# One written order for a fused attention and two-MoE kernel, with subtractions placed one by one and the last output tile sent in halves

## The chip, the cores and the metric

The kernel runs on one core of a Trainium2 chip. The metric is device time in microseconds, the median of repeated executions. The engines named below are TensorE (PE; its weight loads are shown as PEld), VectorE (DVE), ScalarE (ACT), GpSimd (POOL) and SyncE (SP), which here only issues DMAs.

## The reference, cut to what matters

Three stages follow one another; q, k, p are scaled by 8 from the drawn inputs.

```
attention   q, k, v: (8 batches, 8 heads, 576, 64); p: (8, 8, 32, 64)
   packed = softmax(p k^T / 8) v
   x = softmax(q packed^T / 8) packed      -> 4608 tokens x 512
first MoE   h = x w_in (512 x 2048);  g = h * sigmoid(1.702 h);  x = g w_out (2048 x 512)
second MoE  out = (silu(x w_gate) * (x w_val)) w_out (512 x 1536, 512 x 1536, 1536 x 512)
```

All of it is float32. The weights arrive as 64-bit words and are converted on the chip.

## The kernel before, in words

**Precision.** A float32 operand is held as two fp32r tiles, a high part and a rest. `high` (L453) is an ACT copy into the high half, `rest` (L456) a subtraction, source minus high, on the engine that it is given. `mm3` (L465) makes one product from three matmuls. So each operand of TensorE costs one ACT copy and one subtraction; the change speaks of these subtractions.

**First part, eight batches.** A batch has 32 units (two halves of 288 tokens, 16 blocks of 128 hidden columns). Unit n runs `p1` (6 matmuls of 288 columns into `h`), `tanh` on ACT, `gate` on VectorE, `hi` (ACT copy to `gh`) and `lo` (the subtraction), and, three units later, `p2` (12 matmuls of 288 columns into the four `acc` banks). Batch b's units run while batch b+1's attention is computed in between: `do_T`, `sc1`, `max1`, `exp1`, `a1T`, `pv`, `sc2`, `max2`, `exp2`, `norm2`, and last `do_z` (L831), eight times: `zm` (4 matmuls of 512 columns into `zp`, from tiles `wh` that `win` loads), `zc` on ACT and `za` on VectorE, which empty the bank, then `zh` and `zl`. `zp` has two PSUM banks, which it shares with attention's other products; `wh` has three buffers. At the end of a half the four `acc` banks are halved into `x` and stored (L900).

**In the same stretch** two blocks of side work prepare the second MoE: the last batch has no attention, and there `sums` (L1046) and `prep` (L991) form sums of weight tiles in `ws` on VectorE, split them and store them (`w5s`, `w2s`).

**Second part.** One tile of 512 tokens is done directly (`single`, L1285), then four pairs of tiles by a scheme with seven products instead of eight. A pair has 12 units: seven products `pr j 0..6` (6 matmuls of 512 columns each into `gv`), and element work c1, e1 ... g2 on ACT and VectorE. Then come 42 steps `pt n`, each in two halves of 3 matmuls into `acc`, on operands made by `hi n`, `lo n` from the tiles that `SUMS` (L928) names for n. `fd` (L1218) empties an `acc` bank, on ACT for its first group and on VectorE for the others; `tr` transposes a finished tile and `od` (L1234) sends a quarter of it. The next pair's inputs are loaded (`lx`) and split (`xa`, `xh`, `xl`) during the `pt` steps.

**What sets the order.** `FIRST` (the opening, to batch 0's end) and `SECOND` (the four pairs) are texts of steps, carried out by `issue` (L1318); while `pin["on"]` holds, each engine keeps the order of the text. Between them, from batch 1's first unit to the end of the direct tile, `pin` is off (L1329 to L1385): a loop calls the steps, `STEADY` says which attention steps go with which unit, and the framework's own scheduler arranges each engine's instructions.

Of the kernel before, what the change touches and what calls it, by code (L numbers as in the profile page):

```python
# [18 lines left out]
FIRST = """  # L19
    load_raw 0; pad_F 0; make_consts; do_T 0 0; do_T 0 1; load_p 0; load_raw 1; do_p; stage in 3; rebias in 3; stage  # L20
    in 2; warm 12; stage out 1; do_T 1 0; do_T 1 1; load_raw 2; rebias in 2; warm 8; warm 2; sc1 0; max1 0; low in 3
    dve; low out 1 dve; exp1 0; warm 8; warm 5; sc1 1; norm1 0; max1 1; stage in 1; rebias in 1; exp1 1; do_T 2 0;
# [7 lines left out]
    store_w 0 sp; low in 4 dve; rebias in 4; oh 0; join out 2; tanh 1; rebias in 8; oh 2; ol 2 pool; join in 4; tanh  # L30
    0; warm 6; zm 2; ol 0 pool; stage in 7; low in 7 act; rebias in 7; gate 1; max2 1 1; hi 1; lo 1 pool; stage out
    3; stage in 9; zh 2; join in 7; p1 3; exp2 1 1; sc2 0 1; gate 0; stage out 7; tanh 3; zl 2 dve; norm2 1 1; low
    in 8 act; join in 8; low out 3 act; p1 2; stage out 6; store_w 2 sp; rebias out 3; join out 3; tanh 2; hi 0; lo
    0 pool; zm 3; zh 3; rebias out 7; gate 2; hi 2; p2 0; stage in 11; low in 9 dve; zl 3 dve; max2 0 1; load_p 1;
    rebias out 6; stage in 10; low in 11 act; rebias in 9; p1 5; stage in 13; gate 3; hi 3; lo 2 pool; p2 2; join in
    9; rebias in 11; stage in 12; join in 11; zm 4; tanh 5; low out 6 act; join out 6; gate 5; p1 6; rebias in 10;
    lo 3 pool; store_w 3 sp; stage out 10; low in 10 dve; zh 4; oh 3; low out 7 dve; stage out 5; oh 6; join in 10;
    ol 3 pool; join out 7; zl 4 dve; p1 4; tanh 4; gate 4; low in 13 act; low in 12 dve; zm 5; p2 3; oh 7; +do_p;
    rebias in 12; join in 12; zh 5; ol 6 dve; stage in 15; hi 4; p2 1; lo 4 pool; zl 5 dve; p1 9; ol 7 pool; tanh 6;
# [5 lines left out]
    act; zh 7; zl 7 dve; oh 4; tanh 7; exp2 0 1; gate 7; load_raw 5; hi 7; ol 10 pool; +do_T 1 0; +do_T 1 1; +sc1 0;
    +max1 0; tanh 11; p1 10; ol 4 pool; ah 1 1; hi 9; stage out 13; rebias out 13; low out 13 act; p2 4; join out
    13; store_w 5 sp; +exp1 0; lo 7 pool; p2 7; rebias out 9; gate 11; norm2 0 1; join out 9; lo 9 pool; stage out
    11; tanh 10; oh 8; hi 11; lo 11 pool; oh 13; load_v 1 0; ol 8 dve; load_raw 6; store_w 6 sp; gate 10; low out 11
    dve; p1 12; ol 13 dve; stage out 15; tanh 12; rebias out 11; join out 11; gate 12; +sc1 1; hi 10; oh 9; ah 0 1;
    +win 0; p1 13; tanh 13; oh 11; ol 11 pool; p2 8; lo 10 dve; hi 12; lo 12 pool; +max1 1; +exp1 1; p1 14; ol 9  # L50
    pool; stage out 12; gate 13; +norm1 0; p2 10; +do_T 2 0; tanh 14; +do_T 2 1; p2 11; +win 2; hi 13; +a1T 0; gate
    14; wch 0; wcl 0 dve; al 0 1 pool; rebias out 12; load_v 1 1; al 1 1 dve; hi 14; rebias out 15; +copy_a1T 0; low
    out 12 dve; join out 12; p2 9; p1 17; low out 15 act; join out 15; oh 12; p1 16; lo 13 dve; +pv 0; ol 12 dve; p2
    13; tanh 16; wch 2; wcl 2 pool; stage out 14; +norm1 1; tanh 17; oh 15; gate 16; +do_D 0 act; +do_E 0; +a1T 1;
    low out 14 act; +copy_a1T 1; rebias out 14; store_w 7 sp; p1 15; tanh 15; +pv 1; +win 1; join out 14; hi 16; ol
    15 pool; wst 2; oh 14; lo 14 dve; gate 15; ol 14 dve; +split_E 0; p1 21; +zm 0 0; hi 15; wch 1; wcl 1 dve; wst
    0; lo 16 dve; +zc 0 0; +za 0 0; p2 12; +sc2 0 0; tanh 21; gate 21; p1 20; lo 15 dve; +win 3; +do_D 1 act; +do_E
    1; hi 21; p2 14; lo 21 pool; +max2 0 0; +raw_ahead 1; gate 17; +zm 0 1; wch 3; p1 22; +win 5; wst 1; +split_E 1;
    +exp2 0 0; wcl 3 dve; +zc 0 1; +raw_ahead 0; +zm 1 0; +zc 1 0; +win 8; +norm2 0 0; +win 4; wst 3; hi 17; +za 1
    0; tanh 22; gate 22; lo 17 pool; wch 5; +za 0 1; tanh 20; p2 15; wcl 5 dve; wst 5; hi 22; +zm 1 1; +zh 0; +zl 0  # L60
    pool; p1 19; lo 22 dve; tanh 19; gate 19; +zc 1 1; +za 1 1; wch 4; p2 16; p2 17; +zh 1; +zm 2 1; wcl 4 dve; gate
    20; p1 18; hi 20; +zl 1 pool; wch 8; wcl 8 dve; +win 6; hi 19; wst 4; +zm 2 0; tanh 18; lo 19 dve; gate 18; +win
    7; +zc 2 0; +za 2 0; wch 6; +win 10; +zc 2 1; p2 22; p1 25; wcl 6 pool; wst 6; p1 23; tanh 23; +do_T 3 0; +do_T
    3 1; lo 20 pool; +za 2 1; +zh 2; gate 23; +sc2 0 1; +max2 0 1; +sc2 1 0; hi 18; p2 21; tanh 25; wst 8; wch 7;
    wcl 7 dve; +zl 2 pool; hi 23; +zm 3 0; lo 23 pool; +max2 1 0; +zc 3 0; +za 3 0; +win 9; p1 26; p2 19; +zm 3 1;
    tanh 26; gate 25; lo 18 pool; gate 26; +zm 4 0; wch 10; +exp2 0 1; wcl 10 dve; hi 26; lo 26 dve; +win 11; wch 9;
    wcl 9 dve; +zc 3 1; p1 24; wst 7; +win 12; tanh 24; wst 9; +zc 4 0; +za 3 1; +zh 3; p2 26; p2 23; wch 11; +sc2 1
    1; wcl 11 pool; +norm2 0 1; +za 4 0; hi 25; lo 25 pool; +ah 0 1; p1 27; gate 24; +exp2 1 0; +zm 4 1; p1 30; hi
    24; lo 24 pool; +max2 1 1; +ah 0 0; +zl 3 dve; +zm 5 0; p2 20; wch 12; wcl 12 pool; +zc 4 1; +za 4 1; +win 13;
# [1350 lines left out]
```

## Time and profile before

| | |
|---|---|
| median of 3 runs | 1626.05 us (1625.08 to 1627.06) |
| the profiled execution | 1625.42 us, span 1623.7 us |
| PE busy | 1591.4 us, 98% |
| DVE, ACT, POOL busy | 81%, 50%, 24% |
| chain that ended last | PE 81%, DVE 8%, issue 4%, DMA 3% |
| DMA | 349.89 MB, mean 215 GB/s |

The span is the time from the first to the last instruction. The profile's busy time of TensorE takes a modelled end for each matmul, longer than the spacing of matmuls that run without a stop. All source lines are L338 in the trace, since one helper records every operation; rows are told apart by the tile names, written out<-in.

### The profile page before, as it was taken

Reading aid. Unit: us, or ns where it says so; the run is one execution under the profiler, and the core shown is the slowest. Engines: PE = TensorE matmul, PEld = TensorE weight load, DVE = VectorE, ACT = ScalarE, POOL = GpSimd, SP = SyncE. Lnnn points to the kernel's source line nnn. Section 1 sums busy time; section 2 is a strip of 40 time slices with the busy share of each in tenths; the row PEclk is TensorE's granted clock in tenths of the full one; section 3 lists DMA queues with packets and bytes.
Section 4 is the critical chain, followed back from the end, with each engine's and each line's share of the span. In section 5 each row is a group of like instructions: output and inputs, shape, how many; then the busy total and the mean of one; then the engine's idle time right before and its main releaser. Section 6 shows DMA issues by size and latency. Waiting matters only on the chain.

```text
span 1623.7 us, 26484 instructions
## 1 busy us (share of the span) xinstructions
PE 1591.4 (98%) x9202; PEld 1421.3 (88%) x9202; DVE 1312.8 (81%) x2356; ACT 803.9 (50%) x1717; POOL 396.4 (24%) x319
## 2 busy tenths in 40 slices
PE   8999999999999999999999999999999999999997
PEld 7799999999999999999988888778887888788886
DVE  7988787777868778688789388899889988998894
ACT  5876667565665756566554222442235222532241
POOL 1333131230312213124231111241114111321142
PEclk9999999999999999999999999999999999999999
DMA  9987657475664747247899485668567866676627
GB/s 311 321 272 231 195 174 247 140 235 156 210 204 150 228 126 241 88 162 257 301 350 351 144 327 190 207 202 259 188 205 222 204 244 198 198 209 225 198 83 167
DMA packets 254565, 349.89 MB, mean 215 GB/s; under 512 B 127968, under 2 KB 169952, under 8 KB 254432
## 3 DMA queue, kind: packets, MB, share of 16 engines
q1 hardware_dynamic: 252320, 347.94, 67.1%
q8 instruction: 73, 1.20, 0.3%
q14 instruction: 60, 0.49, 0.1%
q10 hardware_dynamic: 2112, 0.26, 0.1%
HBM read 274.20 MB, written 73.92 MB: 214 GB/s over the span
## 4 chain that ended last, share of the span: by engine, by line
PE 81%; DVE 8%; issue 4%; DMA 3%; ACT 2%; SPq 1%; POOL 1%; ACTq 0%; POOLq 0%; DVEq 0%
PE acc L338 32%; PE gv L338 30%; PE h L338 10%; PE sc L338 3%; PE zp L338 3%; PE pv L338 2%; DVE z L338 1%; DMA x<-x2d 1%; DVE g L338 1%; DVE gh L338 1%; PE idle L338 1%; SPq L338 1%; DVE c L338 1%; ACT z L338 1%; DVE x L338 1%
## 5 line engine op out<-in xcount | busy, mean ns | idle before, releaser
L338 PE MATMUL gv<-xh,w 128*128 128x512 f32 x2304 | 537.8, 389 | 0.8 <-DMA w<-w2s 0.8
L338 PEld LDWEIGHTS gv<-xh,w 128*128 128x128 f32 x2304 | 432.3, 188 | 90.9 <-DVE c L338 1.2
L338 PE MATMUL acc<-gh,wo 128*128 128x288 f32 x3072 | 456.1, 297 | 2.6 <-DVE x L338 2.2
L338 PEld LDWEIGHTS acc<-gh,wo 128*128 128x128 f32 x3072 | 426.4, 189 | 7.4 <-DVE x L338 2.4
L338 POOL TENSOR_TENSOR gh<-g,gh 128x512 fp32r<-128x512 f32 (+1 forms) x124 | 171.2, 1384 | 556.6 <-ACT gh L338 485.6
L338 ACT CAST gh<-g 128x288 fp32r<-128x288 f32 (+1 forms) x418 | 208.1, 505 | 163.7 <-DVE g L338 118.2
L338 PE MATMUL h<-a,z 128*128 128x288 f32 x1536 | 252.2, 299 | 1.2 <-DVE g L338 1.0
L338 PE MATMUL acc<-gh,w 128*128 128x512 f32 x972 | 236.7, 390 | 6.1 <-ACT c L338 3.8
L338 DVE TENSOR_TENSOR gh<-g,gh 128x288 fp32r<-128x288 f32 (+1 forms) x294 | 192.8, 656 | 54.0 <-ACT gh L338 50.8
L338 PEld LDWEIGHTS h<-a,z 128*128 128x128 f32 x1536 | 221.0, 189 | 10.4 <-DVE g L338 3.2
L338 PEld LDWEIGHTS acc<-gh,w 128*128 128x128 f32 x972 | 181.5, 188 | 47.6 <-ACT c L338 5.2
L338 DVE TENSOR_TENSOR c<-gv,c 128x512 f32<-128x512 f32 x192 | 131.7, 688 | 20.2 <-ACT tb L338 11.9
L338 DVE SCALAR_TENSOR_TENSOR g<-sig,h 128x288 f32<-128x288 f32 x256 | 114.0, 446 | 36.6 <-ACT sig L338 33.8
L338 ACT ACTIVATE sig<-h 128x288 f32<-128x288 f32 x256 | 104.2, 408 | 68.9 <-PE h L338 66.7
L338 ACT COPY tb<-gv 128x512 f32<-128x512 f32 x48 | 28.2, 587 | 202.7 <-PE gv L338 202.7
L338 POOL TENSOR_TENSOR z<-z,z 128x512 fp32r<-128x512 f32 x51 | 69.7, 1368 | 150.9 <-ACT z L338 150.9
L338 DVE TENSOR_TENSOR z<-zp,z 64x512 f32<-64x512 f32 (+1 forms) x120 | 81.9, 683 | 14.1 <-ACT z L338 11.2
L338 DVE TENSOR_TENSOR ta<-gv,c 128x512 f32<-128x512 f32 x96 | 65.8, 685 | 20.9 <-PE gv L338 20.6
L338 ACT COPY c<-gv 128x512 f32<-128x512 f32 x48 | 28.2, 587 | 107.4 <-PE gv L338 92.5
L338 PE MATMUL zp<-wh,E 128*128 128x512 f32 x224 | 66.7, 400 | 4.4 <-DVE z L338 2.4
L338 ACT COPY z<-zp 64x512 f32<-64x512 f32 x112 | 65.1, 581 | 11.6 <-PE zp L338 8.9
L338 DVE TENSOR_TENSOR g<-g,g 128x512 f32<-128x512 f32 x96 | 68.2, 741 | 0.1
(153 smaller groups left out, 1735.8 us busy)
## 6 DMA issues: line engine op xcount, KB each, us to landing
w<-w2s SPq DMA_DIRECT2D x144, 512.0 KB, 4.4
wh<-win SPq DMA_DIRECT2D x96, 512.0 KB, 4.1
w<-w5s SPq DMA_DIRECT2D x84, 512.0 KB, 4.4
w2s<-w SPq DMA_DIRECT2D x36, 512.0 KB, 5.6
w<-w2s SPq DMA_DIRECT2D x48, 256.0 KB, 2.7
vt<-in_v_dram SPq DMA_DIRECT2D x80, 128.0 KB, 3.3
x2d<-x SPq DMA_DIRECT2D x16, 576.0 KB, 3.2
w2d<-f SPq DMA_DIRECT2D x36, 256.0 KB, 3.0
```

The source lines that it names most:

```text
L338: x = getattr(self.engine, name)(*a, **k)
```

## The change

`STEADY` and the loops go. `FIRST` stays as it was but for the halving and the store of batch 0's first half, which now stand as steps of their own. Twelve further texts, `REST`, hold 5,633 steps: seven for batches 1 to 7, one for the direct tile and four for the pairs. Each step names whose it is (`a3.` is batch 3's attention, `p0.` the first pair), and all are pinned. To make that possible the helpers are cut into single steps: `split_T` into `th` and `tl`, `combine` into four `cb`, `sums` into `sq`, `sh`, `sl`, `sd`, `prep` into `wh2`, `wl2`, `wd2`, the halving into `hv` and its store into `sx`, `single` into `sg`, `st2`, `su2`, `sm2`, `gh2`, `gl2`. The code of each is what stood in the helper, and each subtraction takes its engine from the text.

Counted over the texts, the subtractions on GpSimd are 19 in a batch's attention before and after (batches 3 to 6), and 24 of the sums and 12 of the direct tile before and after; in a pair's first 12 `lo` they were all on GpSimd and are now 5 or 6 on GpSimd and 6 or 7 on VectorE. The same matmuls are made, but for the last output tile.

`SUMS` changes its order, and the last tile has half steps:

```
-    SUMS = [(j % 2, j // 2) for j in range(NM2)] + [(j, k) for j in range(2, 7) for k in range(NK)]
+    SUMS = [(j % 2, j // 2) for j in range(NM2 - 4)] + [(j, k) for j in range(2) for k in range(NK - 2, NK)] + \
+        [(j, k) for j in range(2, 7) for k in range(NK)]
...
+        def pth(n, h):
+            k = n - 36
+            if (k, h) == (0, 0):
+                ab[1] = ps_acc.tile([P, 512], F32, tag="acc1", name="acc")
+            w, y, s = w5[p, n // 2][:, n % 2], oper[p, n], slice(256 * h, 256 * h + 256)
+            mm3(ab[1][:, s], lambda a: w[:, a, P:2 * P], lambda c: y[:, c, s], k == 0, k == NK - 1)
+
+        def fdh(h):
+            s = slice(256 * h, 256 * h + 256)
+            fold(where(6, 1)[0][:, s], ab[1][:, s], c2[:, s])
...
-        def od(j, e, a):
+        def od(j, e, a, eng, h=None):
...
-                    eng = ACT if p == NPAIR - 1 and j == 6 and a % 2 else SP
                     eng.dma_start(out=out[b * S:(b + 1) * S].rearrange("(i n) e -> i n e", n=NBLK)[:, k:k + c, e0:e0 + 32],
                                   in_=y[:, t:t + c])
```

With `SUMS` as it is now, group 0 of the `pt` steps ends at n=9 and group 1 at n=11; before, they ended at n=10 and n=11. Group 2 begins at n=12 in both.

The texts at the places that matter (before, then after; the owner, such as `p0.`, is left out of the pairs' new texts):

```
-    28: "do_z 4; win 13; win 14",
-    30: "do_z 5",
-    31: "do_z 6; win 15; do_z 7",
...
+    a2.win 11; a2.zc 4 0; a2.ah 1 1; a2.za 4 0; a2.al 1 1 pool; a2.zm 4 1; gate 61; a3.do_T 1 1; p1 62; a2.win 12;
+    a2.zc 4 1; hi 61; a2.zm 5 0; a2.za 4 1; a3.raw_ahead 2; p2 59; ...
+    p1 64; lo 63 pool; a2.zm 5 1; p2 61; ... p1 66; ... a2.zm 6 1 ... p1 67; ... a2.zm 7 0; ... a2.zm 7 1; ... p1 68;
...
+    p1 243; hv 239 1 dve; lo2 1; hv 239 0 act; hv 239 2 act; hv 239 3 dve; sh 4 2; lo 242 dve; p2 240; sx 239; ...
...
+    sd 5 2; sh 5 1; oh2 2; cb 0 2; sl 5 1 pool; od2 1; p2 244; ol2 2 dve; tanh 247; sd 5 1; gate 247; sh 5 0;
...
-    pr 11 6; hi 11; xa 0 0; lw5 8; hi 14; b5 11; lx 5; xh 0 4; lo 14 dve; lo 11 pool; pt 10 0; ... pt 10 1; fd 0 0;
-    e5 11; pt 11 0; t2 11; ... pt 12 0; lw5 9; lo 15 pool; fd 0 1; hi 16; pt 12 1;
+    pt 9 1; hi 11; b5 11; lx 5; fd 0 0; pr 11 6; ... pt 10 0; ... e6 11; ... pt 11 0; t2 11; ... pt 12 0; fd 0 1; lw5 9;
+    hi 16; pt 12 1;
...
-    lx 6; pt 26 0; hi 30; lw5 16; lx 7; pt 26 1; xa 1 0; pt 27 0; ... pt 28 0; xh 1 6; lw5 17; hi 32; pt 28 1; xa 1 1;
+    lx 6; fd 3 0; pt 26 0; xl 0 5; lw5 16; hi 30; lx 7; ... pt 29 1; xh 1 4; lo 32 dve; lo 33 pool; xh 1 6; pt 30 0; ...
+    pt 33 0; hi 37; xa 1 1;
...
-    fd 6 1; od 6 0 0; od 6 0 2; tr 6 1; od 6 1 0; od 6 1 1; od 6 1 2; od 6 1 3
+    pth 41 0; od 5 1 3 act; fdh 0; od 6 0 0 sp; pth 36 1; tr 6 1 0; pth 37 1; od 6 0 1 act; od 6 0 2 sp; pth 38 1;
+    od 6 0 3 act; pth 39 1; od 6 1 0 sp 0; pth 40 1; od 6 1 1 act 0; pth 41 1; od 6 1 2 sp 0; od 6 1 3 act 0; fdh 1;
+    tr 6 1 1; od 6 1 0 sp 1; od 6 1 1 act 1; od 6 1 2 sp 1; od 6 1 3 act 1
```

The weight loads of the first pair (`lw 0 0` to `lw 2 1`) stand in the new text ahead of the stores of the direct tile's output; before, `lw 1 0` and the following stood behind them.

## Rows read from the trace of the kernel before

**Rows 1.** The page: busy time, share of the span, instructions of each engine.

```profile
PE 1591.4 (98%) x9202; PEld 1421.3 (88%) x9202; DVE 1312.8 (81%) x2356; ACT 803.9 (50%) x1717; POOL 396.4 (24%) x319
```

**Rows 2.** Windows: stretch, its length, busy us of each engine, clock, DMA.

```profile
148.10:240.00 91.90, 88.68 (x648) 85.90 (x647) 70.45 (x161) 53.08 (x127) 17.98 (x16) 1.00 0.61 182
240.00:760.00 520.00, 517.38 (x3795) 507.57 (x3794) 401.13 (x876) 325.52 (x767) 123.94 (x104) 1.00 0.58 186
760.00:795.00 35.00, 32.09 (x213) 31.01 (x212) 27.33 (x55) 19.18 (x50) 15.73 (x19) 0.90 0.87 299
...
919.00:935.00 16.00, 15.17 (x68) 12.23 (x67) 8.87 (x14) 4.32 (x8) 1.81 (x1) 1.00 0.76 250
...
1050.00:1095.00 45.00, 42.99 (x186) 34.23 (x185) 42.89 (x54) 22.04 (x38) 20.26 (x14) 1.00 0.70 209
1095.00:1225.00 130.00, 130.00 (x575) 107.64 (x574) 110.86 (x164) 38.96 (x68) 19.17 (x13) 1.00 0.70 216
1225.00:1260.00 35.00, 32.81 (x144) 26.50 (x143) 32.81 (x40) 19.48 (x34) 17.23 (x12) 1.00 0.72 220
...
1400.00:1435.00 35.00, 33.17 (x145) 26.85 (x144) 33.16 (x41) 19.02 (x33) 18.55 (x13) 1.00 0.70 210
```

**Rows 3.** Waits of PE, 148.1 to 1615: us in total, times, longest.

```profile
PE acc L338 <- ACT c L338: 3.8, 3, 1.3
PE zp L338 <- DVE z L338: 2.4, 4, 1.1
...
PE acc L338 <- DVE gh L338: 2.0, 3, 0.9
PE zp L338 <- DMA wh<-win: 1.7, 4, 0.7
```

**Rows 4.** Timeline and one window around 780: start, us, instruction, idle before it.

```profile
755.40 1.75 PE L338 MATMUL acc<-gh,wo 128*128 128x288 f32 x12
...
779.95 1.82 DVE L338 TENSOR_TENSOR ws<-w 128x256 f32<-128x256 f32 x2 [0.45 <-POOL tb L338]
...
783.79 2.53 PE L338 MATMUL acc<-gh,wo 128*128 128x288 f32 x9 [2.19 <-DVE x L338]
787.55 2.83 PE L338 MATMUL acc<-gh,wo 128*128 128x288 f32 x12
...
785.00:790.00 5.00, 5.00 (x23) 5.00 (x23) 4.40 (x11) 2.36 (x5) 0.00 (x0) 0.51 0.80 238
```

**Rows 5.** Timeline, 919 to 931: the first pair's weights.

```profile
919.81 9.00 PE L338 MATMUL gv<-xh,w 128*128 128x512 f32 x39
...
923.00 2.31 SPq L338 DMA_DIRECT2D out_dram<-g  x5
...
929.65 5.72 PE L338 MATMUL gv<-xh,w 128*128 128x512 f32 x24 [0.83 <-DMA w<-w2s]
```

**Rows 6.** Timeline, 1226 to 1260: the second pair's pt steps.

```profile
1226.81 0.60 ACT L338 ACTIVATE c<-acc 128x512 f32<-128x512 f32 x1
...
1252.17 0.62 ACT L338 CAST xh<-x 128x512 fp32r<-128x512 f32 x1 [2.89 <-DMA x<-x2d]
```

**Rows 7.** DVE groups, 1095 to 1225: busy us, mean ns, idle before.

```profile
L338 DVE TENSOR_TENSOR c<-gv,c 128x512 f32<-128x512 f32 x48 | 32.9, 688 | 5.0 <-ACT tb L338 3.1
...
L338 DVE TENSOR_TENSOR c<-c,tb 128x512 f32<-128x512 f32 x12 | 15.8, 1313 | 0.0
```

**Rows 8.** The tail: timeline, SP's waits from 1610, time to landing.

```profile
1614.71 0.69 DVE L338 SCALAR_TENSOR_TENSOR ws<-acc,c 128x512 f32<-128x512 f32 x1 [2.64 <-PE acc L338]
1615.43 0.71 DVE L338 STREAM_TRANSPOSE g<-ws 128x512 f32<-128x512 f32 x1
...
1615.88 5.45 SPq L338 DMA_DIRECT2D out_dram<-g  x9
...
SPq L338 <- DMA out_dram<-g: 4.0, 3, 2.7
...
DMA to landing us min/median/max: 1.3/1.8/2.1
```

More of the change, by code (lines that the diff above doesn't have):

```diff
@@ L30 @@
[L30 to L39, printed above, removed]
@@ L45 @@
[L45 to L54, printed above, removed]
@@ L55 @@
[L55 to L69, printed above, removed]
@@ new lines @@
+    a0.norm2 0 1; join out 9; lo 9 pool; stage out 11; tanh 10; oh 8; hi 11; lo 11 pool; oh 13; load_v 1 0; ol 8
+    dve; load_raw 6; store_w 6 sp; gate 10; low out 11 dve; p1 12; ol 13 dve; stage out 15; tanh 12; rebias out 11;
+    join out 11; gate 12; a1.sc1 1; hi 10; oh 9; a0.ah 0 1; a1.win 0; p1 13; tanh 13; oh 11; ol 11 pool; p2 8; lo 10
+    dve; hi 12; lo 12 pool; a1.max1 1; a1.exp1 1; p1 14; ol 9 pool; stage out 12; gate 13; a1.norm1 0; p2 10;
+    a1.do_T 2 0; tanh 14; a1.do_T 2 1; p2 11; a1.win 2; hi 13; a1.a1T 0; gate 14; wch 0; wcl 0 dve; a0.al 0 1 pool;
@@ L723, in do_D @@
             st["pvp", g] = ps
-            if not whole:
-                do_E(g)
         def do_E(g):
@@ L829, in zl @@
             rest(z[b, n % 2, n // 2], st["z32", n], eng)
-        def do_z(n):
-            for c in range(2):
-                zm(n, c)
-                zc(n, c)
-                za(n, c)
-            zh(n)
-            zl(n)
         def raw_ahead(n):
@@ L907, in p2, with hv, sx @@
             mm3(acc[e][:, :HS], lambda a: wo[m][:, a, e * P:(e + 1) * P], lambda c: y[:, c], m == 0, m == NM - 1)
-        if m == NM - 1:
-            x = m1.tile([P, NE, HS], F32, tag="x2", bufs=1, name="x2")
-            for e in range(NE):
-                halve(x[:, e], acc[e][:, :HS], e % 2)
-            c0 = b * S + t * HS
-            SP.dma_start(out=x2d[:, :, c0:c0 + HS].rearrange("e p t -> p e t"), in_=x)
+    def hv(n, e, eng):
+        if n not in x2:
+            x2[n] = m1.tile([P, NE, HS], F32, tag="x2", bufs=1, name="x2")
+        halve(x2[n][:, e], acc[e][:, :HS], eng is DVE)
+    def sx(n):
+        c0 = units[n][0] * S + units[n][1] * HS
+        SP.dma_start(out=x2d[:, :, c0:c0 + HS].rearrange("e p t -> p e t"), in_=x2.pop(n))
     NPAIR = NB2 // 2
@@ L1316, with space, issue @@
     engines = dict(dve=DVE, pool=POOL, act=ACT, sp=SP)
-    def issue(text, ops, ops_next=None):
+    spaces = {}
+    def space(x):
+        if x not in spaces:
+            spaces[x] = dict(a=attention, p=pair)[x[0]](int(x[1:]))
+        return spaces[x]
+    def issue(text):
         for x in text.split(";"):
             f, *a = x.split()
-            f = ops_next[f[1:]] if f[0] == "+" else ops[f]
-            f(*[int(c) if c.isdigit() else engines.get(c, c) for c in a])
-    ops = dict(attention(0), load_p=load_p, load_raw=load_raw, load_v=load_v, make_consts=make_consts, stage=stage,
+            w, _, f = f.rpartition(".")
+            f = space(w)[f] if w else ops[f]
+            f(*[int(c) if c.lstrip("-").isdigit() else engines.get(c, c) for c in a])
@@ L1362 @@
-    act2(units[-1])
-    for n in range(len(units) - LAG, len(units)):
-        p2(units[n])
-    m1.release()
-    open_m2()
-    steps = x_steps(0)
-    for i in range(8):
-        load_x2(0, i)
-    for m in range(NM2):
-        single(m, m - 2)
-        for part in range(4):
-            if m:
-                prep(m + 1, part)
-        if m == NM2 - 1:
-            load_w(NM2)
-            fill(m - 1)
-        for _ in range(2):
-            if steps and (len(steps) > 4 or m == NM2 - 1):
-                steps.pop(0)()
@@ L1381 @@
-    fill(NM2 - 1)
-    while steps:
-        steps.pop(0)()
-    open_g()
-    pin["on"] = True
-    for p, text in enumerate(SECOND):
-        issue(text, pair(p), pair(p + 1))
+               hi=lambda n: hi(units[n]), lo=lambda n, eng: lo(units[n], eng), p2=lambda n: p2(units[n]), hv=hv, sx=sx,
+               begin2=begin2, second2=second2, third2=open_g, gv=load_gv, lf=lf, fh=fh, fl=fl, cb=cb, wh2=wh2, wl2=wl2,
+               wd2=wd2, lo2=load_wo2, oh2=oh2, ol2=ol2, od2=od2, ls=ls, sq=sq, sh=sh, sl=sl, sd=sd, sg=sg, st2=st2,
@@ L1388 @@
+               su2=su2, sm2=sm2, gh2=gh2, gl2=gl2, p5=p5, hv5=hv5, so=so)
+    issue(FIRST)
+    for text in REST:
+        issue(text)
     pools2["m"].release()
```

1159 lines of the change are left out of this document (754 added, 405 removed), and 28 rows, old and new, of the table STEADY.

## The prediction

> **What bounds the kernel.** I read the page's busy times first: TensorE is busy 98% of the span and no other engine over 81% [rows 1]. So only two things can shorten this kernel without removing matmuls, and the change removes none: time in which TensorE stands still, and the ends of the span, where it has nothing to do yet or any more. The opening keeps its text, so I left it out. Next I cut the rest into windows and took length minus busy time of TensorE. The idle time is not spread evenly: 3.22 us in 148 to 240, 2.62 in 240 to 760, 2.91 in 760 to 795, 0.83 at 919, and 2.01, 2.19 and 1.83 at one place in each of three pairs, where the `pt` steps begin [rows 2]. The sum is 15.6 us. Between these places it runs without a gap (130.00 of 130 us in 1095 to 1225 [rows 2]). So the question is what each gap waits for and whether the written order takes that away.
>
> A gap costs more than its idle time, since the busy time has modelled ends. At 919.81 a run of 39 matmuls begins. At the undisturbed spacing of 130/575 = 0.226 us [rows 2] the fortieth would start at 928.63; it starts at 929.65 [rows 5], 1.02 late for 0.83 idle. So about 0.19 us goes to refilling. The dearest waits are 14, and those at 783 and 929 make 16 [rows 3 to 5]: 16 x 0.19 = 3.0 us. One gap costs still more. Behind the wait of 2.19 us at 783.79 the granted clock is 0.51 in 785 to 790, that is 1.2 GHz in place of 2.4, and 12 matmuls take 2.83 us where the same 12 took 1.75 [rows 4]: 0.09 each, and some 27 matmuls run at that pace (0.09 x 27 = 2.4 us). All that can be won after 148 us is thus 15.6 + 3.0 + 2.4 = 21.0 us.
>
> **The change part by part.**
>
> *The ends of the batches* (5.84 us idle). TensorE waits there for `zp` banks that VectorE's `za` has yet to empty (2.4 us, 4 times) and for `wh` tiles on their way (1.7 us, 4 times) [rows 3]. Both come from eight `do_z` crowded into a batch's last units: each `zm` needs a bank that the one before it has just filled, and its `win` came moments before. The new texts carry `zm` 5 1 to 7 1 over into the next batch, one in a unit, and set each `win` one to six units ahead of its `zm`, mostly two or three. Neither wait then has much of a cause. What is late next is `sc1` of the following attention, which moves back by the same units and has most of a batch to catch up. I leave 0.5 us.
>
> *760 to 795* (2.91 us idle, 2.4 of clock). VectorE's two subtractions of `sums` took 1.82 us and had waited 0.45 for a GpSimd subtraction of `tb`; the halving into `x` stood behind them, and TensorE behind the halving [rows 4]. The new text puts the four `hv`, two of them on ACT, ahead of `p2 240` and of the next `sq`, and one `sq` in half a unit instead of four together. I leave 0.3 us, and with no gap of that size the clock has nothing to fall after.
>
> *919* (0.83). The weights of the first pair stand behind stores of the direct tile on SP's queue (5 issues, 2.31 us [rows 5]). In the new text the loads go first. I leave nothing; the stores have the whole pair.
>
> *Three pairs* (6.03 us idle). TensorE waits for the ACT copy that empties group 1's `acc` bank (3.8 us in 3) and for `gh` (2.0 in 3) [rows 3]. The copy itself takes 0.60 us [rows 6], so it is late by its place in ACT's queue. `SUMS` now ends group 0 one step earlier, `pr 11 6` is set between that and the next group, and group 1's `fd 0 1` has a longer stretch. The `gh` is late because ACT stood 2.89 us for an `x` tile that had been asked for moments before [rows 6], with `hi` queued behind it. The new text sets that `xh` about eight half steps of 0.226 x 3 = 0.68 us later, 5.4 us. I leave 0.2 us a pair, 0.6 in all.
>
> *The moved subtractions.* In a pair 6 of 12 `lo` go from GpSimd to VectorE. Bounds by rows: 6 x 0.688 = 4.1 us more of VectorE at most [rows 7]; and less than nothing at best, because 12 of VectorE's operations on two tiles beside them take 1313 ns, not the 688 of the form that reads one operand from a bank [rows 7]: if each of the 6 frees one of these, 6 x 0.625 = 3.8 us come back. Either way VectorE was busy 110.86 of 130 us [rows 2], so TensorE covers it, and I take nothing. If the cover were gone, 4.1 us a pair would be at stake, 16 in all.
>
> *The tail.* The last matmul ends at 1614.7. Then come a fold of 0.69 and a transpose of 0.71 us over the whole tile, and SP issues until 1621.33, held up by landings of earlier stores (4.0 us in 3); the span ends at 1623.7 [rows 8], which leaves about 2.4 us behind the last issue. That is 9.0 us behind TensorE. In the new text only half of the tile is left by then. Fold and transpose of half the columns have no row; between 0.70 (all in proportion) and 1.40 (nothing saved) I take 0.8, near the lower end, since fold and transpose, two different operations, take the same time for 512 columns, as if the columns alone counted. Four issues on two queues: two each, 2 x 0.45 = 0.9 (2.31/5 [rows 5]). Behind them 2.4 as before. Together 4.1, so 4.9 saved. The last group is cut into twice as many matmuls, 18 more: nothing at the least, 0.9 at most (the mean spacing of the smaller matmuls in 240 to 760 is 520/3795 = 0.137 us [rows 2]; twice that less 0.226, times 18), I take 0.4. Net 4.5. If SP still waits once for a landing of 2.7 [rows 8], 1.9 remain; the best is 5.6. The Trainium skill, "Trainium Kernel Development and Optimization", section Key Constraints, holds that transfers of all queues share the same engines and that several issuers save only issue time; by that, with the waits for landings staying, the sum would have the 1.9 for this term. The trace agrees as far as a landing after an issue takes 1.3 to 2.1 us here.
>
> **The sum.** 21.0 - 0.5 - 0.3 - 0 - 0.6 = 19.6 from the middle, 4.5 from the tail: 1625.4 - 24.1 = 1601.3 us on the profiled execution. The median stands 0.6 above that execution; waits too short to have a row of their own pull the other way by about as much. I say 1601. A measurement of this kernel can tell about 0.2%, 3.3 us, from no change.
>
> **Rivals.**
>
> *A, the forecast*: 0.62. Its own range is 1594 to 1608. Low: the whole 21.0 and 5.6 of the tail give 1598.8, and refilling known from one place could be 0.5 instead of 0.19 (16 x 0.3 = 4.8). High: the tail gives 1.9 and 4 us more stay of the middle.
>
> *B, the gaps move*: 0.22. For the middle's batches the framework's scheduler ordered each engine by itself; a written order also fixes what it got right. The first units of a batch now hold `zc`, `za` and four `hv` beside `tanh`, `gate` and `hi`. If at six batch starts one wait of the longest kind seen for `zp` appears (1.1 + 0.19 [rows 3]) and 0.7 at each of three pairs, 7.7 + 2.1 = 9.8 us of the gain are gone: 1611. Against it: VectorE is 77% and ACT 63% busy in 240 to 760 [rows 2], with room for it.
>
> *C, the middle stays*: 0.08. If the waits follow from buffers (two `zp`, three `wh`) and not from order, only the tail changes: 1620.9. Against it: the waits are a few places and not every batch unit.
>
> *D, VectorE falls behind GpSimd*: 0.08, and slower. With every order fixed, a VectorE operation that needs a `tb` or `gh` from GpSimd, or that stands behind one that does, can't be passed by. The row at 779.95 shows that this costs TensorE 2.19 us, and with 0.19 for refilling and 2.4 for the clock 4.8 us [rows 4]. It decides from six such places (24.1/4.8 = 5.02); at seven the time is 1601.3 + 33.6 = 1635. For it: VectorE is at 42.89 of 45 us where the `pt` steps begin [rows 2], so a delay there isn't absorbed. Against it: GpSimd is busy 24% [rows 1], and half of the pair's `lo` leave it. The Trainium skill, "SBUF — State Buffer", section Who interferes with whom, says that a VectorE instruction with two SBUF inputs contends with a GpSimd instruction that reads SBUF, and that the one that issues second is blocked; 1313 against 688 ns [rows 7] agree in direction. By that rule every GpSimd subtraction set beside such an operation would bring a place of D nearer.
>
> **Chances and range.** Faster: A and B, and C for the part of it beyond 3.3 us (0.05): 0.89. Same: the rest of C and the mild end of D: 0.05. Slower: 0.06. The range of 1594 to 1614 holds A and most of B, about 8 in 10.
>
> **What would show it.** No wait for `zp` on `wh` or `z` among TensorE's longest; the granted clock 1.00 all through 760 to 795; no wait on `w2s` at the first pair; the waits on ACT's `c` gone or under 0.3; VectorE's two-tile mean below 1313 ns in a pair; 4 us from TensorE's last matmul to the end. I am wrong if new waits stand at batch starts (B), if a second stretch at half clock appears (D), or if SP still waits for landings (the tail).

## The result, and the profile after

The changed kernel takes 1608.07 us (median of 4 runs, 1607.60 to 1609.27) against 1626.55 of the kernel before beside it: ratio 0.9886, 95% interval 0.9869 to 0.9903. That is 18.5 us less, inside the range of 1594 to 1614; 1601 was said. The profiled execution has a span of 1606.1 us, 17.7 less than the span of 1623.7 before. In experiment 3 below one execution of four, the profiled one, took 3204 us, twice as long as the others; the number given there is the median of the other three.

The page's busy times (they answer to [rows 1]), and windows of four stretches: batch 1, batches 2 to 6, the stretch around 780, and the first pair (they answer to [rows 2]; length, then busy us of TensorE, weight loads, VectorE, ACT, GpSimd, then clock and DMA).

```profile
PE 1586.3 (99%) x9220; PEld 1420.2 (88%) x9220; DVE 1342.2 (84%) x2383; ACT 809.3 (50%) x1719; POOL 343.4 (21%) x292
```

```profile
147.68:245.25 97.57, 94.63 (x699) 92.57 (x697) 79.53 (x172) 58.24 (x141) 18.59 (x16) 1.00 0.68 195
245.25:730.91 485.66, 482.78 (x3533) 471.26 (x3531) 382.27 (x824) 304.18 (x713) 110.71 (x92) 1.00 0.60 179
760.00:795.00 35.00, 35.00 (x267) 35.00 (x266) 27.53 (x53) 21.63 (x56) 17.17 (x21) 1.00 0.83 281
912.02:1083.57 171.55, 171.55 (x757) 141.85 (x756) 149.90 (x213) 62.02 (x107) 29.33 (x21) 1.00 0.67 215
```

The reader sees two kernels in one. Around 780 and in the pair TensorE stands still no more and the clock is at its full level; in the batches 2.94 and 2.88 us of idle time are left. Before, batch 1 had 3.22 us of it (99.44 less 96.22), and batches 2 to 6 had 2.04, by their window in the kernel before:

```profile
247.54:730.64 483.10, 481.06 (x3534) 472.28 (x3533) 370.91 (x825) 302.10 (x713) 112.52 (x93) 1.00 0.58 182
```

TensorE makes the same matmuls in both kernels but for the last tile, so the two traces can be cut at the same matmuls: the first of units 32, 64 and 224, the first of the direct tile, the first of each pair, the last of all. The forecast's terms are set beside the differences (refills of 0.19 us, the prediction's price of starting TensorE again behind a wait, with their waits).

| stage | before, us | after, us | difference | forecast |
|---|---|---|---|---|
| opening | 148.10 | 147.68 | -0.4 | 0 |
| batch 1 | 99.44 | 97.57 | -1.9 | together |
| batches 2 to 6 | 483.10 | 485.66 | +2.6 | -6.9 |
| last batch | 90.54 | 83.19 | -7.3 | -5.2 |
| direct tile | 97.94 | 97.92 | 0.0 | 0 |
| pairs 1 to 3 | 523.64 | 514.37 | -9.3 | -7.6 |
| pair 4 | 171.91 | 174.46 | +2.6 | +0.4 |
| behind the last matmul | 9.04 | 5.20 | -3.8 | -4.9 |
| sum (the span) | 1623.71 | 1606.05 | -17.7 | -24.1 |

Between the cuts three of the stages don't hold quite the same work: of the 512-column matmuls into `zp`, batch 1 has 22 and not 24, batches 2 to 6 have 160 and not 162, and the last batch has 10 and not 6. At 0.226 us each, the same work took -1.4, +3.0 and -8.3 us.

A second trace of the changed kernel gave 97.54, 485.33, 83.19, 97.92, 514.23, 174.31 and 5.05. How well a stage repeats is seen from the runs below that leave its text as it is: the last batch always took 83.19 us and the direct tile 97.9, batches 2 to 6 took 485.3 to 486.6. The opening took 146.5 to 149.7, pair 4 173.1 to 174.7, and pair 4 with the stretch behind it 178.2 to 179.9. So the runs below are read by stages, against these spreads; most of their times, which carry the opening, differ by less than the intervals.

TensorE's waits from 148 to 1600 us (total, times, longest; they answer to [rows 3]):

```profile
PE zp L692 <- DVE z L692: 3.2, 3, 1.5
PE acc L692 <- ACT x L692: 1.0, 5, 0.2
PE h L692 <- DVE a L692: 1.0, 1, 1.0
PE acc L692 <- ACT c L692: 0.8, 1, 0.8
PE acc L692 <- DMA w<-w5s: 0.6, 1, 0.6
PE acc L692 <- DVE ws L692: 0.5, 1, 0.5
PE h L692 <- DVE g L692: 0.2, 1, 0.2
```

The waits on `wh`, on `gh`, on the weights at the first pair and the three on ACT's `c` are gone (the one on `c` here stands in pair 4, at a place that had none). Of the waits on `z`, three stand here at other steps, and those on `x` and `a` are new. The `z`, `x`, `a` and `g` lie in the batches: 5.4 us up to 760 us, as much as before. There it was 2.4 and 1.7 for `zp` [rows 3], and two waits in the middle of batch 1 that [rows 3] doesn't show:

```profile
PE sc L338 <- ACT a L338: 0.7, 1, 0.7
PE sc L338 <- POOL pb L338: 0.6, 1, 0.6
```

The tail (timeline and SP's waits; they answer to [rows 8]):

```profile
1591.58 12.27 SPq L692 DMA_DIRECT2D out_dram<-g  x17
...
1600.88 0.42 DVE L692 SCALAR_TENSOR_TENSOR ws<-acc,c 128x256 f32<-128x256 f32 x1 [2.03 <-PE acc L692]
1601.35 0.45 DVE L692 STREAM_TRANSPOSE g<-ws 128x256 f32<-128x256 f32 x1
...
SPq L692 <- DMA out_dram<-g: 5.2, 5, 3.1
```

Fold and transpose end at 1601.80, SP's last issue at 1603.85.

How a wait in the batches arises, in the timeline of the changed kernel near 204 us, in the middle of batch 1:

```profile
202.77 0.76 DVE L692 TENSOR_TENSOR Th<-T,Th 128x576 fp32r<-128x576 f32 x1
202.86 1.96 POOL L692 TENSOR_TENSOR Th<-T,Th 128x576 fp32r<-128x576 f32 x1 [17.95 <-DVE gh L692]
...
204.86 0.78 DVE L692 STREAM_TRANSPOSE T<-raw 128x576 f32<-128x576 f32 x1 [1.33 <-POOL Th L692]
...
205.56 0.41 DVE L692 SCALAR_TENSOR_TENSOR g<-sig,h 128x288 f32<-128x288 f32 x1
...
206.01 0.43 ACT L692 CAST gh<-g 128x288 fp32r<-128x288 f32 x1 [2.21 <-DVE g L692]
...
206.35 0.70 ACT L692 ACTIVATE x<-acc 128x288 f32<-128x288 f32 x2
...
206.80 2.00 PE L692 MATMUL acc<-gh,wo 128*128 128x288 f32 x12 [0.21 <-ACT x L692]
```

A transposition on VectorE waits 1.33 us for a GpSimd subtraction; the gate behind it is late, so ACT's `gh` is, so the halving `x` behind that one is, and TensorE waits for the bank. Three queues in a fixed order pass the delay on.

The longer waits on `z` (1.53 us at 240 and 1.43 at 717) have two causes in the text. The second of them in the timeline:

```profile
715.29 0.43 ACT L692 CAST gh<-g 128x288 fp32r<-128x288 f32 x1 [2.10 <-DVE g L692]
...
716.06 0.58 ACT L692 COPY z<-zp 64x512 f32<-64x512 f32 x1
716.11 0.46 DVE L692 TENSOR_TENSOR x<-x,sm 128x288 f32<-128x288 f32 x1
716.61 0.48 DVE L692 STREAM_TRANSPOSE xT<-x 128x288 f32<-128x288 f32 x1
...
717.12 0.69 DVE L692 TENSOR_TENSOR z<-zp,z 64x512 f32<-64x512 f32 x1
...
717.86 0.72 PE L692 MATMUL zp<-wh,E 128*128 128x512 f32 x2 [1.43 <-DVE z L692]
```

The bank is emptied by `zc` on ACT and then by `za` on VectorE. The `zc` at 716.06 stands behind a `hi` (`gh<-g`) for which ACT waited 2.10 us, and `za` begins 0.48 us behind the end of `zc`, after attention's `x` and `xT`.

### The profile page after: what moved, and what is told of

It is laid out like the page before. It is cut to its first block, busy times and chain, and to the rows that moved or that the text cites. A ratio compares the mean times of both kernels' runs of the same rounds, so it can differ in the third digit from the quotient of the medians.

```text
span 1606.1 us, 26623 instructions
## 1 busy us (share of the span) xinstructions
PE 1586.3 (99%) x9220; PEld 1420.2 (88%) x9220; DVE 1342.2 (84%) x2383; ACT 809.3 (50%) x1719; POOL 343.4 (21%) x292
## 4 chain that ended last, share of the span: by engine, by line
PE 83%; DVE 10%; ACT 3%; issue 2%; DMA 1%; POOL 1%; SPq 0%; ACTq 0%; DVEq 0%; POOLq 0%
PE acc L692 34%; PE gv L692 32%; PE h L692 9%; PE sc L692 3%; PE pv L692 2%; PE zp L692 2%; DVE z L692 2%; DVE g L692 1%; DVE gh L692 1%; DVE sm L692 1%; DVE x L692 1%; ACT z L692 1%; PE idle L692 1%; POOL Th L692 1%; PE a1T L692 1%
## 5 line engine op out<-in xcount | busy, mean ns | idle before, releaser
L692 POOL TENSOR_TENSOR gh<-g,gh 128x512 fp32r<-128x512 f32 (+1 forms) x105 | 132.5, 1265 | 605.3 <-ACT gh L692 571.9
L692 PE MATMUL h<-a,z 128*128 128x288 f32 x1536 | 248.6, 297 | 2.2 <-DVE a L692 1.0
L692 DVE TENSOR_TENSOR gh<-g,gh 128x288 fp32r<-128x288 f32 (+1 forms) x313 | 188.0, 605 | 37.4 <-ACT gh L692 34.3
L692 POOL TENSOR_TENSOR z<-z,z 128x512 fp32r<-128x512 f32 x46 | 62.1, 1350 | 143.4 <-ACT z L692 136.3
L692 ACT ACTIVATE s<-c 128x512 f32<-128x512 f32 x48 | 30.4, 633 | 69.1 <-DVE c L692 69.1
```

The lines of the kernel that those rows point to most:

```text
L692: x = getattr(self.engine, name)(*a, **k)
```

## The experiments

Each is the changed kernel with the edit shown. Ratios are to the kernel before, run beside it.

**1. The last tile whole.**

```diff
-    pth 36 0; fd 6 0; pth 37 0; ... fdh 0; ... pth 36 1; tr 6 1 0; ... fdh 1; tr 6 1 1; od 6 1 0 sp 1; ...
+    pt 36 1; fd 6 0; pt 37 1; ... pt 41 1; ... fd 6 1; tr 6 1; od 6 1 0 sp; od 6 1 1 act; od 6 1 2 sp; od 6 1 3 act
```

> The changed kernel, but the last output tile is computed, folded, transposed and sent whole, as in the kernel before; its stores stay divided over two queues. If the halves are worth what the prediction gave them (4.5 us), or at least what the trace of the changed kernel suggests (the stretch behind TensorE's last matmul fell from 9.0 to 5.2 us, less 0.7 us for the wait of the second half's first matmul on the first half's fold), this run takes 3 to 4.5 us more than the changed kernel: about 1611.5. Rival: the gain at the tail came from dividing the stores over the two queues and not from the halves; then it takes at most 1.5 us more.

1606.53 us, ratio 0.9876 (0.9862 to 0.9891). Pair 4 took 172.60 (not 174.46) and the stretch behind it 6.19 (not 5.20): together 178.8, 0.9 us less than the changed kernel, within the spread of 178.2 to 179.9, and not 3 to 4.5 more. So the halves bring up to 1.0 at the end and cost as much ahead of it. The first expectation fell; the rival's bound of at most 1.5 us held. Without the halves the tail is still 6.19 and not 9.04 us. What is left of the change there is that the stores, all but four of them SP's before, are divided over two queues, and that two of them (`od 6 0 0`, `od 6 0 2`) stand ahead of the last fold and not behind it. No run tells the two apart. The Trainium skill, "Trainium Kernel Development and Optimization", section Key Constraints, grants several issuers only issue time; the trace agrees, since the last stores of the changed kernel land no sooner after their issue (medians of 1.6 to 2.2 us by the size of the store) than those before (1.5 to 1.9).

**2. The second half in another PSUM bank.**

```diff
+            if (k, h) == (0, 1):
+                ab[3] = ps_acc.tile([P, 512], F32, tag="acc3", name="acc")
-            mm3(ab[1][:, s], ...
+            mm3(ab[1 + 2 * h][:, s], ...
```

> The changed kernel with the second half of the last output tile in another PSUM bank. If the wait of 0.52 us of the second half's first matmul (and 0.16 of refill) comes from the first half's fold reading the same bank, it goes: 0.7 us less. Rival: the fold's end is needed for another reason (the operands); then nothing changes.

1606.91 us, ratio 0.9878 (0.9864 to 0.9893). TensorE's timeline in the changed kernel, then here:

```profile
1594.10 3.81 PE L692 MATMUL acc<-xh,w 128*128 128x512 f32 x24 [0.57 <-DMA w<-w5s]
...
1598.43 2.42 PE L692 MATMUL acc<-xh,w 128*128 128x256 f32 x18 [0.52 <-DVE ws L692]
```

```profile
1592.69 8.58 PE L692 MATMUL acc<-xh,w 128*128 128x512 f32 x54
```

The wait on the fold is gone: the theory held. The wait for `w5s` went too in this run, but that is not the edit's doing: in runs with the same text at that place it lies between nothing and 1.02 us. SP issues that load behind stores, some of which wait for landings; whether this makes the spread wasn't tried. Pair 4 took 172.84, 1.6 us less than in the changed kernel, but the stretch behind it took 6.09, 0.9 more, since SP's last store came only 0.7 sooner: together 178.9, within the spread. The 36 smaller matmuls take about 2 x 2.42 us where 18 whole ones take 18 x 0.226 = 4.07: 0.8 more, near the bound of 0.9.

**3. A transposition behind the gate, five places.**

```diff
-    a3.do_T 0 0; tanh 50; gate 50;
+    tanh 50; gate 50; a3.do_T 0 0;
```

> The changed kernel with one step moved at five places: the transposition of the next batch's first tile (do_T 0 0) stands behind gate 50 (82, 114, 146, 178) and not ahead of it. In the changed kernel VectorE waits 1.33 us there for a GpSimd subtraction that still reads the tile, the gate, the hi and the halving of acc behind it come late, and TensorE waits 0.21 us and then refills for about 0.4 us. If the place of that one step in VectorE's fixed order is the cause, the five waits on ACT's x go and about 0.6 x 5 = 3 us with them: 1605. Rival: the halving is late because only one unit lies between the end of a half and the next half's first matmul; then nothing changes.

1606.30 us (1604.71 to 1607.17), ratio 0.9872 (0.9855 to 0.9888); there is no trace to read by stages. The time doesn't decide between the two expectations: the changed kernel has a ratio of 0.9886 and, in experiment 11, 0.9874. But the same edit stands in experiment 4, with no other exchange near it. In its trace none of the five places idles, and TensorE gets from unit 50 to unit 53, and likewise at the other four, 0.33 to 0.36 us sooner. So the place of that step is the cause, and the five waits cost 1.7 us and not 3.

**4. Steps exchanged at 16 places of the first part** (the five above and, for example):

```diff
-    a3.norm2 1 1; a3.zc 4 1; ... tanh 94; a3.za 4 1; a3.ah 1 1; a3.zm 5 0; gate 94; a3.al 1 1 pool; a3.zh 4;
+    a3.zc 4 1; ... tanh 94; a3.za 4 1; gate 94; a3.zm 5 0; a3.norm2 1 1; a3.zh 4; a3.ah 1 1; a3.al 1 1 pool;
```

> The changed kernel with steps exchanged at 16 places of the first part and no engine changed: al 1 0 of batch 1 ahead of two zl; the transposition behind the gate (five places); za 4 0, za 4 1 and za 2 1 ahead of the subtraction, the transposition and the norm2 of attention that stood before them (two places); the gate ahead of norm2 at a batch's last but one unit (four); zh 6 on ACT behind the halvings (five). If the idle time that stayed between 148 and 760 us is VectorE's and ACT's written order, waiting steps ahead of steps that TensorE needs, the waits on zp (3.2 us), on a (1.0), on x (1.0) and on g go, and with the refills 7 to 9 us: span about 1598. Rival: these engines are simply late there, and the waits return at the next step: less than 3 us.

1604.96 us, ratio 0.9866 (0.9851 to 0.9880). Batch 1 took 96.92 and batches 2 to 6 484.70: 1.6 us less, not 7 to 9 (at least 1.2 less than any trace with the changed kernel's text). TensorE's waits from 148 to 770 us:

```profile
PE zp L681 <- DVE z L681: 2.5, 4, 1.0
PE acc L681 <- ACT x L681: 1.1, 4, 0.3
PE h L681 <- DVE g L681: 0.9, 3, 0.4
PE sc L681 <- DVE Th L681: 0.4, 1, 0.4
```

The five waits in the middle of the batches are gone, and so is that on `a`; but 4.9 us are there again, at other steps. The rival is nearer the truth: what lets one step go ahead makes another late. Unit by unit, the four exchanged gates gave 1.6 us at their place, and 0.9 of it went again four to nine units on, where TensorE now waits for the halvings (`x`). The two long waits on `z` are 0.73 us at 239 and 0.97 at 715, and not 1.53 and 1.43: `za` stands ahead of attention's steps here, but `zc` is late on ACT as before.

**5. The pairs' first 12 subtractions on GpSimd.**

```diff
-    p1.lo 0 dve;
+    p1.lo 0 pool;
```

(26 such subtractions in the four pairs.)

> The changed kernel with all of the first 12 lo of each pair on GpSimd again, as before (26 subtractions go back). The prediction gave their move no time, since TensorE covers VectorE: within 1 us of the changed kernel, with VectorE's operation on two tiles (c<-c,tb) back from 1042 to about 1313 ns. Rival: in the fixed order VectorE is held up beside every GpSimd subtraction, and TensorE waits where the pt steps begin: 1.5 to 6 us slower (0.4 to 1.5 a pair).

1607.21 us, ratio 0.9876 (0.9862 to 0.9891). Pairs 1 to 3 took 514.51 and pair 4 174.03: no difference to speak of, the prediction's nothing held. Over the four pairs the operation on two tiles has a mean of 1252 ns here, 1024 in the changed kernel and 1198 in the kernel before (the 1313 and 1042 are those of one stretch): the expected direction and nearly the size. In pair 4 the wait of 0.77 us on ACT's `c` is gone. That the edit did it isn't shown: it is gone in experiment 6 too, whose pairs have the changed kernel's text.

**6 to 8. The halving of the last batch late.** First behind two sums, of which one waits for GpSimd:

```diff
-    p1 243; hv 239 1 dve; lo2 1; hv 239 0 act; hv 239 2 act; hv 239 3 dve; sh 4 2; lo 242 dve; p2 240; ...
+    p1 243; lo2 1; sh 4 2; sl 4 2 pool; lo 242 dve; sq 4 3; sq 5 2; hv 239 0 act; hv 239 1 dve; ... p2 240; ...
```

> The changed kernel with the four halvings of the last batch's first half behind two sums of VectorE, of which the second waits for a GpSimd subtraction, as it stood in the kernel before. If that order made the wait of 2.19 us and the half clock behind it, both come back: TensorE idle 1.5 to 2.5 us near 780 and then a granted clock below 1, 3 to 5 us in all: 1611 to 1613. Rival 1: the clock fell for another reason; then only the idle time and its refill come, 1.7 to 2.7 us. Rival 2: VectorE catches up before TensorE needs the banks: nothing changes.

1608.53 us, ratio 0.9888 (0.9872 to 0.9905); TensorE waited 0.82 us for VectorE's `x`, the last batch took 84.30 (not 83.19), the clock stayed at 1.00. That is 1.1 us, less than the first two expectations, more than the last. Then behind three sums:

```diff
+    ... sh 4 1; sl 4 1 pool; sq 4 3; sq 5 2; sq 5 0; hv 239 0 dve; hv 239 1 dve; hv 239 2 act; hv 239 3 act; p2 240; ...
```

> As the run before with the late halvings, but behind three sums, of which two wait for GpSimd subtractions. TensorE should now stand still for about 2 us near 781, as in the kernel before. If the long wait lowers the clock, the granted clock is near 0.5 for some 6 us behind it and the whole costs 5 to 7 us against the changed kernel; if the clock had another cause (the attention of the last batch, transfers), it stays at 1.00 and the whole costs 2.2 to 2.7 us.

1609.25 us, ratio 0.9890 (0.9876 to 0.9905); last batch 85.85. TensorE's timeline, and windows:

```profile
780.20 1.86 PE L690 MATMUL acc<-gh,wo 128*128 128x288 f32 x12 [2.39 <-DVE x L690]
```

```profile
778.00:780.00 2.00, 0.00 (x0) 0.00 (x0) 1.38 (x5) 1.07 (x4) 1.03 (x2) 1.00 0.46 148
780.00:782.00 2.00, 1.80 (x13) 1.83 (x14) 1.24 (x4) 0.43 (x1) 0.00 (x0) 1.00 0.31 111
782.00:784.00 2.00, 2.00 (x17) 2.00 (x16) 0.60 (x2) 1.14 (x3) 0.00 (x0) 1.00 1.12 334
```

The wait is longer than the 2.19 us of [rows 4], and the clock doesn't fall: 2.66 us lost, the second expectation, of which 0.27 are the refill. Last, with the first halving ahead, so that three matmuls stand between two waits, as before:

```diff
+    ... sh 4 1; hv 239 0 act; lo 242 dve; sl 4 1 pool; sq 4 3; sq 5 2; sq 5 0; hv 239 1 dve; hv 239 2 dve; hv 239 3 act; ...
```

> As the run with the halvings behind three sums, but the first of the four halvings stands on ACT ahead of them, so that TensorE does three matmuls and then waits for the second bank, as in the kernel before. In the run without this split a wait of 2.39 us left the granted clock at 1.00. If what counts is that TensorE had little to do over the whole stretch ahead of and behind those three matmuls, the clock falls to about 0.5 here for some 6 us, and the stage of the last batch takes 5 to 7 us more than in the changed kernel. If a single wait can't do it at this place, the clock stays at 1.00 and the stage takes 2 to 2.7 us more.

1609.76 us, ratio 0.9898 (0.9883 to 0.9913). The waits came out as 0.83 and 0.81 us, the last batch as 85.36 (2.2 more), the clock at 1.00: the second expectation, but with waits unlike the 0.31 and 2.19 us before, so that it doesn't decide.

**9. The pairs' old texts** (`SECOND` and `SUMS` of before, the direct tile's stores behind the first weights):

```diff
-    SUMS = [(j % 2, j // 2) for j in range(NM2 - 4)] + ...
+    SUMS = [(j % 2, j // 2) for j in range(NM2)] + ...
```

> The changed kernel with the four pairs' texts and SUMS of the kernel before (the direct tile's stores stay in the first pair's text, the weights ahead of them), so also the old tail. By the prediction's terms 6.6 us (pairs) and 4.5 us (tail) are lost: 11 us more than the changed kernel. By the two traces the pairs gave 8, the last pair's new waits took 2.3 and the tail gave 3.8: 9.5 us more. Rival: the pairs' waits in the kernel before were left over from the direct tile's late start (0.83 us at 919); then the waits on ACT's c stay away here and it is under 6 us.

1616.76 us, ratio 0.9940 (0.9924 to 0.9957): by the stages 7.0 us more than the changed kernel (pairs 1 to 3 5.0, pair 4 -1.8, tail 3.8), less than both sums. By the medians it is 8.7 more, and 10.5 more than in experiment 11, so how much less isn't settled; more than the rival's 6 it is. TensorE's waits from 912 to 1600 us, and ACT's longest two waits for `x` at the second pair:

```profile
PE acc L450 <- ACT c L450: 3.8, 3, 1.3
PE acc L450 <- DMA w<-w5s: 0.4, 1, 0.4
PE acc L450 <- DVE gh L450: 0.2, 1, 0.2
```

```profile
1241.89 0.62 ACT L450 CAST xh<-x 128x512 fp32r<-128x512 f32 x1 [1.39 <-DMA x<-x2d]
1244.74 0.62 ACT L450 CAST xh<-x 128x512 fp32r<-128x512 f32 x1 [1.18 <-DMA x<-x2d]
```

The three waits on `c` are back to the tenth: they come from the pair's old text with the old `SUMS`, which were not tried one by one. The waits on `gh` (2.0 us in [rows 3]) are back by a tenth only: ACT waits at most 1.94 us for `x` here (at the first pair) and not 2.89 [rows 6], and that hardly reaches TensorE. The old order makes ACT wait. How long goes with the landing of the load: at the second pair the two loads took 5.8 us (median) before and 4.8 here. Why they land sooner here isn't known.

**10. All of it together** (the gates and transpositions of 4, a new order of units 60 to 62 and 215 to 219, 5, 1 with two more stores on ACT and the last weight load ahead of a store).

> The changed kernel with what the runs so far pointed to: the exchanges of steps in the first part that shortened it (the transposition behind the gate, the gate ahead of norm2, al ahead of zl), zc on ACT ahead of a hi that waits and norm2 behind the gates near 240 and 717 us; the first 12 lo of a pair on GpSimd; the last tile whole, two more stores on ACT's queue and the last weight load ahead of a store. By the stages of the runs: 4 us from the batches 1 to 6 (2.3 for five transpositions, 1.6 for four gates), up to 3 more near 240 and 717 if the waits don't come back, 2 from the last pair and 0.5 at the tail: span 1597 to 1600 (with the opening as in the changed kernel). Rival: VectorE and ACT are late in the batches whatever the order, and only the pairs' 2 us come: 1604.

1608.00 us, ratio 0.9886 (0.9870 to 0.9903), span 1606.4: neither expectation. Pair 4 and the tail gave 1.6 us, batch 1 (96.30) gave 1.3, but batches 2 to 6 took 488.72, 3.1 more than in the changed kernel. One place of its timeline tells why:

```profile
720.63 0.48 DVE L673 STREAM_TRANSPOSE xT<-x 128x288 f32<-128x288 f32 x1
721.15 0.43 ACT L673 CAST a<-xT 128x288 fp32r<-128x288 f32 x1 [2.44 <-DVE xT L673]
721.60 0.41 ACT L673 ACTIVATE sig<-h 128x288 f32<-128x288 f32 x1
...
722.04 0.46 DVE L673 SCALAR_TENSOR_TENSOR g<-sig,h 128x288 f32<-128x288 f32 x1 [0.93 <-ACT sig L673]
...
722.55 0.66 PE L673 MATMUL h<-a,z 128*128 128x288 f32 x3 [2.54 <-DVE g L673]
```

At four batch starts TensorE also waits 0.57 to 0.79 us for ACT's `x`. And at this place `norm2` was put behind the gate on VectorE, as meant. But the `ah` that needs it stayed ahead of a `tanh` on ACT; ACT waits 2.44 us, the next gate for it, TensorE 2.54.

**11. The changed kernel again**, beside 10.

> The changed kernel itself once more, beside the others on one chip: 1608 within 1 us; its stages as in its first trace, within 0.3 us each but for the opening.

1606.23 us, ratio 0.9874 (0.9859 to 0.9888): 21.0 us less than the kernel before beside it, where the first measurement had 18.5. It lies 1.8 us below 1608, and the expected 1 us was too narrow: two measurements of one kernel differ by that much here. The stages repeated as expected (those of the second trace above).

**12. What had held**: as 10, but units 215 to 219 as in the changed kernel, and `zh 6` behind the halvings as in 4.

> The changed kernel with only those exchanges that shortened a stage in the runs so far: the five transpositions behind the gate, al ahead of zl, the new order of units 60 to 62, the four gates together with the zh 6 behind the halvings; units 215 to 219 left as they are in the changed kernel (their new order brought a wait of 2.54 us); the pairs' first 12 lo on GpSimd and the last tile whole with its stores spread, as in the run with all three. From the stages: batch 1 96.3, batches 2 to 6 482.4, the last batch, the direct tile and the pairs 767.4, tail 6.3, opening 147.5: span 1600. Rival: the exchanges' gains don't add, since what one lets go ahead is late at the next step; then batches 2 to 6 stay above 484 and the span above 1601.5.

1603.80 us, ratio 0.9868 (0.9849 to 0.9887), span 1601.6: batch 1 96.25, batches 2 to 6 484.12, pairs 514.51 and 171.69, tail 6.30. The batches and the span are where its rival put them (above 484 and 1601.5): the gains don't add. The wait on `z` at 240 is gone, here and in experiment 10, where `zc` stands ahead of the `hi` (among other exchanges there); that at 715, where units 215 to 219 are as in the changed kernel, is 1.42 us. Its span is the shortest here, 4.4 us under the first trace of the changed kernel and 3.3 under the second (1604.9); by its ratio it can't be told from experiment 4 (0.9866).

## Why the prediction was right, point by point

- **TensorE is the bound, and its gaps are the stock to win**: right. It is busy 99% after. Of the 17.7 us, 12.5 are idle time of TensorE, the ends included; the other 5.1 are busy time, 2.9 of them the half clock.
- **The ends of the batches** ("I leave 0.5 us"): the step that failed. Forecast 6.9 us less; measured -1.9 + 2.6, so that batches 1 to 6 are 0.7 us longer, for the same work 1.6. To their ends belong also two waits that stand behind the cut, at 731 and 733 us (0.38 and 0.20 us, 1.2 with what follows them), and they are gone: +0.4 us in all. The mechanism was right for `wh`, whose waits are gone. Wrong was "Neither wait then has much of a cause": for `zp` other causes stood in the same text, `za` behind attention's steps on VectorE and `zc` behind a waiting `hi` on ACT (240 and 717 us), and the steps beside the moved ones were not followed (`x` in the middle of five batches, `a` at 149). That is rival B, though only `a` stands at a batch's start, where B was put, and in part rival D: at the five places a VectorE step waits 1.33 us for GpSimd. Experiment 4 shows that place as the cause, experiments 4, 10 and 12 that such waits then turn up elsewhere. The reading of the stock was off too: 1.3 of the 5.84 us were the two waits on `sc` in the middle of batch 1. Open stays why batches 2 to 6 are 3.0 us longer for the same work, when only 0.8 of that are idle time.
- **760 to 795**: right, mis-sized. The stage's -7.3 us are, unit by unit, 7.1 here and 1.2 at 731 and 733, less 0.9 for the four more matmuls: 7.1, not 5.2. The idle 2.91 us are four waits (0.20, 0.22, 0.31, 2.19), and the 27 slow matmuls took 6.43 us (783.79 to 790.22) where 27 x 0.132 = 3.6 are normal (12 took 1.58 at 793): 2.9 and not 2.4. The other 1.3 are four refills of 0.3 and not one of 0.19. That a late halving makes such a wait is shown by experiments 6 and 7. Why the clock fell isn't (below).
- **919**: right. No wait on `w2s` is left.
- **Three pairs**: right, mis-sized: 9.3 with the 919, not 7.6. Nothing was left of the 0.6 that I kept, and the term that was too small is the refill: idle time was 6.87 of the 9.3 us, as read, and the other 2.4 make 0.3 for each of eight waits (three on `c`, three on `gh`, two on weights). Experiments 6 to 8 gave 0.27 to 0.29 a wait. Experiment 9 shows the old text with its `SUMS` as cause for the waits on `c`; for those on `gh` only in part.
- **The moved subtractions**: right, nothing (experiment 5).
- **The tail**: right in direction, its step wrong. 3.8 us came behind the last matmul, not 4.9, and pair 4 lost 2.6, not 0.4: 0.8 for smaller matmuls, 0.52 of idle time for a fold in the same bank, 0.57 for `w5s` and 0.77 for `c`, which is not the tail's. The fold and transpose of half the columns took 0.92, near the 0.8. But SP went on waiting for landings, so its last store was issued 2.05 us behind the transpose, not 0.9. Experiment 1: the halves bring nothing that can be told from the spread; the stores' new order on two queues does. The best case of 5.6 doesn't come out of the term's own numbers (9.0 - 0.70 - 0.9 - 2.4 = 5.0); only the low end of the range rests on it.
- **Range and chances**: the time lies between the end of A's own range (1608) and B's 1611, in experiment 11 within A's, for the reason the two give: A's gaps went in the second part, B's moved in the first. That it came so near to 1601 is in part luck: the batches fell 7.3 us short of the forecast and the tail 3.2, and 760 to 795 and the pairs gave 3.6 more than forecast, because refills and half clock cost more than the prediction's prices. Of its signs of being wrong, SP's waits for landings came (5.2 us in 5), and of the new waits at batch starts one, on `a`.

## What to carry to other kernels

Before costing a stall that a new order takes away, name for each moved step what stands behind it on its own engine, and what stands ahead of the step that feeds it: a fixed order passes a delay from queue to queue (VectorE, ACT, TensorE), and taking a step ahead only helps if the step that feeds it doesn't block a third queue. Measure the price of a restart at several waits: 0.19 us from one place was 0.3 in the pairs and around 780. Cut both traces at the same matmuls, count what lies between the cuts, and compare stages: a total that fits can hide a stage that got slower. And try the order of a tail's stores and their queues before smaller pieces: here they took 9.0 us to 6.2, while the halves won nothing that could be told from the spread.

## What was not expected of the hardware

The clock: in the kernel before, 2.19 us without work were followed by 6 us at half clock (0.51, that is 1.2 GHz) [rows 4]; in experiment 7 a wait of 2.39 us at the same place left it at 1.00. Before that fall TensorE had also idled 0.31 us with three matmuls between:

```profile
780.94 0.66 PE L338 MATMUL acc<-gh,wo 128*128 128x288 f32 x3 [0.31 <-ACT x L338]
```

In the run that tried this (8) the waits were shorter. What decides stays open.

Two subtractions at once, in the changed kernel's timeline:

```profile
234.46 1.31 POOL L692 TENSOR_TENSOR z<-z,z 128x512 fp32r<-128x512 f32 x1 [1.65 <-ACT z L692]
234.50 1.57 DVE L692 TENSOR_TENSOR a<-xT,a 128x288 fp32r<-128x288 f32 x1
```

VectorE's took 1.57 us, begun 0.04 us behind GpSimd's and ended 0.30 behind it; alone the same one takes 0.44 (experiment 4's trace, 246.01). The Trainium skill, "SBUF — State Buffer", section Who interferes with whom, says that the later one is blocked until the earlier one is done; the trace agrees. The written order sets the two at one place here. It stands 6 us ahead of the wait of 1.53 us on `z`; whether it makes that wait wasn't tried.
